# A recurrent attention state and an MLP on one core: the last 64 rows of x multiplied on the two row halves of TensorE

## The chip, the cores and the metric

The kernel runs on one core of one Trainium2 chip. The metric is device time in microseconds (us). Before the change the median of 3 runs is 756.64 us.

## What is computed

For 4 x 8 batch-head pairs a 40 x 40 state is updated 768 times; its outputs, put side by side, are x with 3072 tokens and 320 features. An MLP follows.

```python
for t in range(S):                       # S = 768, state is B x H x 40 x 40
    y[:, :, t] = einsum('bhd,bhde->bhe', rt, state)
    Sa = einsum('bhde,bhe->bhd', state, at)
    state = state * wt - outer(Sa, bt) + outer(vt, kt)
x = y.transpose(0, 2, 1, 3).reshape(3072, 320)
h = x @ w_in                             # 320 -> 2048
sp = maximum(h, 0) + log1p(exp(-abs(h)))
out = (h * erf(sp)) @ w_out              # 2048 -> 320
```

## The kernel before

**The recurrence** is cut into chunks of 32 steps: 48 chunk steps in all (2 groups of 16 heads, 24 chunks each), computed with small matrix products. A chunk step issues on TensorE, under the names used below: A (line 484, 104 rows contracted, 64 output columns), two sets of transposes (502, 664), Z (639, 96 x 32), U (648, 32 x 32), one more transpose (673), PQ (682, 104 x 64), MY (693 and 697, 64 x 40 and 40 x 40, on the row halves and the column halves of the array, into the two PSUM banks of `my`). For each group of four chunks there are W and DAD (595, 32 x 32). All of these but the transposes use a part of the array, and many of them share it. Each instruction carries the shape of tile into which it divides the array: 128 x 64, 128 x 32, 64 x 64 or 32 x 32 for A and PQ, Z, MY, and U, W and DAD; the whole 128 x 128 for the transposes and for the MLP's products. "Small tile" below means any shape other than 128 x 128.

**The MLP** runs in 12 tiles of 256 tokens (`load_x`), each in 8 pieces n (`mm1`, `unit`, `post`). A piece is a pair of blocks of 128 columns of w_in: 256 of the 2048 columns. So there are 96 pieces and 192 blocks. x and w_in are split in a high and a low part (`xh` + `xl`, `wih` + `wil`), and a block sums three products: high by high, high w by low x, low w by high x. The 320 rows of x are two sets of 128 and a rest of 64. For the rest, `wir` (128 x 2048) holds the high part of w_in's last 64 rows in partitions 0 to 63 and the low part in 64 to 127, and `xh[2]` holds the rest of x twice, so one full matmul gives high by high and low by high together. `xl[2]` is the low part of the rest; its partitions 64 to 127 are zeros, written once at the start (line 420).

So a block (line 869) is 8 matmuls of 128 x 128 weights by 256 columns, in one accumulation:

```python
ops = [(s.wih[0], xh[0], 128), (s.wih[1], xh[1], 128), (s.wir, xh[2], 128), (s.wih[0], xl[0], 128),
       (s.wih[1], xl[1], 128), (s.wir, xl[2], 128), (s.wil[0], xh[0], 128), (s.wil[1], xh[1], 128)]
```

The sixth, `wir` by `xl[2]`, is the one with zeros in half of its rows. The pieces take the two PSUM banks `ph[0]` and `ph[1]` in turn; a copy (`hc`, mostly ScalarE, line 376) takes the bank to `h` in SBUF. After Tanh, Ln, Exp and Gelu on ScalarE and products on VectorE, `post` multiplies by w_out (line 924): 4 products of 128 x 128 by 320 columns for each piece, 384 in all, into `po`. They are fp32, and the trace has two records for each of them, and also for each fp32 product of the recurrence; the matmuls of line 869 are float32r and have one.

**The order** of all work is a table of numbers, `ORDER`, with a second one, `ENGINES`, that gives each operation its engine. `Plan.add` lists operations with what they read and write, `emission` issues them in the table's order, and each engine runs its own instructions in that order. On TensorE blocks of line 869, products of line 924 and the small tiles of the recurrence stand mixed. After the program proper stands a second, sequential form of the recurrence, which runs only if a flag is set; it isn't in the trace.

Of the kernel before, what the change touches and what calls it, by code (L numbers as in the profile page):

```python
# [1056 lines left out]
```

## Time and profile before

| what | value |
|---|---|
| three runs | 752.92, 757.29, 756.64 us; median 756.64 us |
| the profiled execution | 755.08 us |
| its span, first to last instruction | 752.8 us |
| mean granted clock of TensorE over the span | 0.985 of full speed |
| busy share of the span | PE 95%, PEld 76%, DVE 85%, ACT 79% |

PE stands for TensorE's matmuls, PEld for its weight loads, DVE for VectorE, ACT for ScalarE. In a row, "start, duration" of a matmul cover its whole way through the array, and consecutive matmuls overlap: what one of them costs TensorE is read from the distance of one end to the next (start plus duration), not from its own duration. Where several like matmuls stand in one row, the row's end is that of the last of them.

### The profile page before, as it was taken

Reading aid. Unit: us, or ns where it says so; the run is one execution under the profiler, and the core shown is the slowest. Engines: PE = TensorE matmul, PEld = TensorE weight load, DVE = VectorE, ACT = ScalarE, POOL = GpSimd, SP = SyncE. Lnnn points to the kernel's source line nnn. Section 1 sums busy time; section 2 is a strip of 40 time slices with the busy share of each in tenths; the row PEclk is TensorE's granted clock in tenths of the full one; section 3 lists DMA queues with packets and bytes.
Section 4 is the critical chain, followed back from the end, with each engine's and each line's share of the span. In section 5 each row is a group of like instructions: output and inputs, shape, how many; then the busy total and the mean of one; then the engine's idle time right before and its main releaser. Section 6 shows DMA issues by size and latency. Waiting matters only on the chain.

```text
span 752.8 us, 32777 instructions
## 1 busy us (share of the span) xinstructions
PE 717.6 (95%) x14131; PEld 574.0 (76%) x14131; DVE 637.2 (85%) x1444; ACT 594.2 (79%) x1179; POOL 3.9 (1%) x12
## 2 busy tenths in 40 slices
...
GB/s 256 180 132 139 197 243 127 142 134 121 127 163 102 138 151 108 132 137 108 140 119 135 123 110 141 131 124 131 122 118 116 110 128 91 100 57 58 26 19 21
DMA packets 157523, 93.31 MB, mean 124 GB/s; under 512 B 107612, under 2 KB 141084, under 8 KB 157372
## 3 DMA queue, kind: packets, MB, share of 16 engines
...
q14 instruction: 38, 0.31, 0.2%
...
## 4 chain that ended last, share of the span: by engine, by line
PE 73%; DVE 9%; ACT 7%; DMA 5%; issue 3%; SPq 1%; DVEq 0%; ACTq 0%
PE po L924 25%; PE ph L869 19%; PE my L693 4%; PE pQ L682 3%; PE pA L595 3%; PE pA L484 3%; PE ph L424 2%; PE my L648 2%; ACT r L877 2%; PE my L639 2%; PE pA L502 2%; PE pQ L664 2%; ACT l L877 2%; PE my L697 2%; SPq L382 1%
## 5 line engine op out<-in xcount | busy, mean ns | idle before, releaser
L924 PE MATMUL po<-wo,h 128*128 128x320 f32 x768 | 267.2, 458 | 2.9 <-issue 2.1
L924 PEld LDWEIGHTS po<-wo,h 128*128 128x128 f32 x768 | 128.0, 192 | 34.5 <-issue 2.8
L869 PE MATMUL ph<-xh,wih 128*128 128x256 f32 x384 | 114.4, 379 | 1.1 <-ACT xh L376 0.6
L877 ACT ACTIVATE l<-l 128x512 f32<-128x512 f32 x192 | 111.2, 624 | 2.5 <-DVE nd L902 1.6
L869 PEld LDWEIGHTS ph<-xh,wih 128*128 128x128 f32 x384 | 69.7, 190 | 25.8 <-ACT xh L376 1.1
L869 PE MATMUL ph<-xl,wih 128*128 128x256 f32 x384 | 77.3, 283 | 0.0
L869 PE MATMUL ph<-xh,wil 128*128 128x256 f32 x384 | 77.0, 282 | 0.0
L902 DVE TENSOR_TENSOR nd<-l,r 128x512 f32<-128x512 f32 x96 | 64.0, 685 | 11.3 <-ACT r L877 9.7
L376 ACT COPY h<-ph 128x512 f32<-128x512 f32 x87 | 50.4, 583 | 26.3 <-PE ph L869 22.1
L914 DVE TENSOR_TENSOR l<-l,r 128x512 f32<-128x512 f32 x96 | 64.3, 682 | 1.1 <-ACT l L877 0.2
L903 DVE SCALAR_TENSOR_TENSOR r<-nd,r 128x512 f32<-128x512 f32 x96 | 64.7, 682 | 0.4
L915 DVE SCALAR_TENSOR_TENSOR h<-l,h 128x512 f32<-128x512 f32 x96 | 64.4, 682 | 0.5
L877 ACT ACTIVATE l<-h 128x512 f32<-128x512 f32 x96 | 58.2, 628 | 5.7 <-DVE h L378 4.2
L869 PEld LDWEIGHTS ph<-xh,wil 128*128 128x128 f32 x384 | 59.7, 191 | 0.0
L869 PEld LDWEIGHTS ph<-xl,wih 128*128 128x128 f32 x384 | 59.3, 190 | 0.1
L877 ACT ACTIVATE r<-r 128x512 f32<-128x512 f32 x96 | 55.7, 625 | 0.5
L869 PE MATMUL ph<-xl,wir 128*128 128x256 f32 x192 | 54.5, 284 | 0.0
L869 PE MATMUL ph<-xh,wir 128*128 128x256 f32 x192 | 54.1, 282 | 0.0
L877 ACT ACTIVATE r<-l 128x512 f32<-128x512 f32 x96 | 53.7, 618 | 0.2
L491 DVE TENSOR_TENSOR Zs<-pA,tri 64x256 f32<-64x256 f32 x96 | 40.6, 423 | 13.5 <-PE pA L484 6.5
L693 PE MATMUL my<-Vu,sg 64*40 64x72 f32 x1536 | 46.2, 230 | 3.8 <-DVE Vu L685 2.4
L693 PEld LDWEIGHTS my<-Vu,sg 64*40 64x40 f32 x1536 | 34.6, 114 | 11.8 <-DVE Vu L685 3.9
...
## 6 DMA issues: line engine op xcount, KB each, us to landing
...
```

The lines of the kernel that those rows point to most:

```text
L376: self.nc.scalar.copy(o, i)
L484: nc.tensor.matmul(pa[i % 2 * 64:i % 2 * 64 + 64, i // 4, i // 2 % 2], bk[:, i].rearrange("p a b -> p (a b)"), ab[:, :, i], start=True, st ...
L491: P.add("Am", "DVE", lambda e, x=x, xs=xs: nc.vector.tensor_tensor(out=zx[64:128, x], in0=pz[xs], in1=s.tri[xs, None, :].to_broadcast([64, ...
L595: nc.tensor.matmul(pw[js, i, ts], l[js, i], r[js, i, ts], start=True, stop=True)
L693: nc.tensor.matmul(my[h * 64:h * 64 + 40, x, j], sg[xs, j, h], vu[xs, j // 2 * 2 + h, j % 2], start=True, stop=False)
L869: nc.tensor.matmul(ph[:, j * 256:j * 256 + 256], a[:k, fs], b[:k], start=(m == 0), stop=(m == 7))
L877: self.P.add(name, "ACT", lambda e: nc.scalar.activation(out=o, in_=i, **kw), rd, wr + ["act"], pr, 0.62)
L902: P.add("nd", [("DVE", 0.69)], lambda e, r=r, l=l, nd=nd: s.eng(e).tensor_tensor(out=nd, in0=l, in1=r, op=ALU.mult), [("l", il), ("r", ir) ...
L903: P.add("rho", "DVE", lambda e, r=r, nd=nd: nc.vector.scalar_tensor_tensor(out=r, in0=nd, scalar=2 * C4, in1=r, op0=ALU.add, op1=ALU.mult) ...
L914: P.add("E", [("DVE", 0.69)], lambda e: s.eng(e).tensor_tensor(out=l, in0=l, in1=r, op=ALU.mult), [("r", ir)], [("l", il)], pr)
L915: P.add("G", "DVE", lambda e: nc.vector.scalar_tensor_tensor(out=h, in0=l, scalar=-1.0, in1=h, op0=ALU.add, op1=ALU.mult), [("l", il)], [( ...
L924: nc.tensor.matmul(po, h[:, bs], s.wo[:, f], start=(f == 0), stop=(f == 15))
```

## The change

`wir` is laid out anew: of the 8 pieces of a token tile, even ones keep high in partitions 0 to 63 and low in 64 to 127, odd ones have low above and high below. `xl[2]` is computed in all 128 partitions, since `xr` holds the rest of x twice, and the zeros of line 420 are gone. A block then has 7 matmuls (line 872 of the changed kernel), and after each even piece an operation of its own, `mk` (line 882), adds high w by low x of the rest for the even piece and the next odd one: 4 matmuls of 64 rows, 128 weight columns and 256 moving columns, in turn on array rows 0 to 63 into `ph[0]` and on rows 64 to 127 into `ph[1]`. Their tile is 64 x 128. `mk` closes the sum in `ph[0]` and opens the one in `ph[1]`.

```diff
@@ host @@
-    o["moe_w_in3"] = np.concatenate([wi[256:320, :1024], wi[256:320, 1024:]])
+    w3 = wi[256:320].reshape(64, 4, 2, 256)
+    o["moe_w_in3"] = np.concatenate([w3[:, :, x].reshape(64, 1024) for x in range(2)])
@@ start @@
-        for j in range(len(s.XL)):
-            P.add("zxl", "ACT", lambda e, j=j: nc.scalar.copy(s.XL[j][2][64:128], zero[64:128, :256]), s.TK, [("xl", j, 2)], -50, 0.36)
@@ weights @@
-                P.add("wr0", "ACT", lambda e, f=f, xs=xs, qs=qs: nc.scalar.copy(s.wir[0:64, qs], f[xs]), [kf], [kr + ("h",)], pr, 0.6)
+                P.add("wr0", "ACT", lambda e, f=f, xs=xs, qs=qs: nc.scalar.copy(s.wir[xs, qs], f[xs]), [kf], [kr + ("h",)], pr, 0.6)
...
@@ load_x @@
-            P.add("xl", [("DVE", 0.42)], lambda e, k=k, raw=raw, n=n: s.eng(e).tensor_tensor(out=xl[k][:n], in0=raw[:n], in1=xh[k][:n].bitcast(F32), op=ALU.subtract), ...
+            P.add("xl", [("DVE", 0.42)], lambda e, k=k, raw=raw: s.eng(e).tensor_tensor(out=xl[k], in0=raw, in1=xh[k].bitcast(F32), op=ALU.subtract), ...
@@ mm1 @@
+        col = lambda t, j: t % 2 * 1024 + t // 2 * 256 + j * 128
+        t, odd = n % 8, n % 2 == 1
...
-                ops = [(s.wih[0], xh[0], 128), (s.wih[1], xh[1], 128), (s.wir, xh[2], 128), (s.wih[0], xl[0], 128), (s.wih[1], xl[1], 128), (s.wir, xl[2], 128), (s.wil[0], xh[0], 128), (s.wil[1], xh[1], 128)]
-                for m, (a, b, k) in enumerate(ops):
-                    nc.tensor.matmul(ph[:, j * 256:j * 256 + 256], a[:k, fs], b[:k], start=(m == 0), stop=(m == 7))
+                ops = [(s.wih[0][:, fs], xh[0]), (s.wih[1][:, fs], xh[1]), (s.wir[:, cs], xh[2]), (s.wih[0][:, fs], xl[0]), (s.wih[1][:, fs], xl[1]), (s.wil[0][:, fs], xh[0]), (s.wil[1][:, fs], xh[1])]
+                for m, (a, b) in enumerate(ops):
+                    nc.tensor.matmul(ph[:, j * 256:j * 256 + 256], a, b, start=(m == 0 and not odd and j == 0), stop=(m == 6 and odd and j == 1))
...
+        if not odd:
+
+            def mk(e):
+                for j in range(2):
+                    for x in range(2):
+                        xs, cs = slice(x * 64, x * 64 + 64), slice(col(t + x, j), col(t + x, j) + 128)
+                        nc.tensor.matmul(s.ph[x][:, j * 256:j * 256 + 256], s.wir[xs, cs], xl[2][xs], start=(x == 1 and j == 0), stop=(x == 0 and j == 1))
+
+            P.add("mk", "PE", mk, xks + wkr(t) + wkr(t + 1) + ["phw"] * (n == 0), [("ph", 0), ("ph", 1)], pr, 0.35)
@@ ORDER and ENGINES, both written anew @@
-2 3 28 29 30 31 32 33 34 35 36 37 38 39 40 41 42 43 44 45 46 47 48 49 50 51 52 53 54 55 56 57 58 59 60 61 62 63 64 65 66 67 68 69 70 6 27 11 7 71 72 73 74 75 76 77 13 78 9 4 17 15
...
```

The order on TensorE, before, at a usual place in the second half: `ph_163` and `ph_164` are `ph[0]` and `ph[1]`, `po_165` and `po_166` the two banks of `po`. A whole block stands between a product of line 924 and transposes of line 664.

```order
L924 MATMUL po_166<-wo,h 128x320
L869 MATMUL ph_164<-xh_0_152,wih_126 128x256
L869 MATMUL ph_164<-xh_1_153,wih_127 128x256
L869 MATMUL ph_164<-xh_2_154,wir 128x256
L869 MATMUL ph_164<-xl_0_158,wih_126 128x256
L869 MATMUL ph_164<-xl_1_159,wih_127 128x256
L869 MATMUL ph_164<-xl_2_160,wir 128x256
L869 MATMUL ph_164<-xh_0_152,wil_128 128x256
L869 MATMUL ph_164<-xh_1_153,wil_129 128x256
L664 MATMUL pQ<-ident,MT_111 104x104 x4
L639 MATMUL my<-Zm_77,Zs_70 32x40 x16
```

In the changed kernel, at a like place of TensorE, `mk` (line 882) stands alone between a product of w_out (line 936 there) and the next block:

```order
L936 MATMUL po_165<-wo,h 128x320
L882 MATMUL ph_163<-xl_2_157,wir 128x256
L882 MATMUL ph_164<-xl_2_157,wir 128x256
L882 MATMUL ph_163<-xl_2_157,wir 128x256
L882 MATMUL ph_164<-xl_2_157,wir 128x256
L872 MATMUL ph_164<-xh_0_149,wih_126 128x256
L872 MATMUL ph_164<-xh_1_150,wih_127 128x256
```

The sixth matmul of a block is gone, and four of another tile shape stand between two runs of whole-array work. At another place of the changed kernel's TensorE, `mk` stands ahead of a small tile of the recurrence, here U of line 648:

```order
L872 MATMUL ph_163<-xh_1_153,wil_129 128x256
L936 MATMUL po_166<-wo,h 128x320
L664 MATMUL pQ<-ident,MT_111 104x104 x4
L639 MATMUL my<-Zm_77,Zs_70 32x40 x16
L936 MATMUL po_166<-wo,h 128x320
L882 MATMUL ph_163<-xl_2_160,wir 128x256
L882 MATMUL ph_164<-xl_2_160,wir 128x256
L882 MATMUL ph_163<-xl_2_160,wir 128x256
L882 MATMUL ph_164<-xl_2_160,wir 128x256
L648 MATMUL my<-zt_110,Tb_83 32x40 x16
L936 MATMUL po_166<-wo,h 128x320
```

Here the array's shape changes from 128 x 128 to 64 x 128, to 32 x 32 and back, where without `mk` it would go to 32 x 32 and back.

Counted over the whole order of TensorE, in matmuls whose tile shape differs from that of the one before:

| change of shape | before | changed |
|---|---|---|
| 128 x 128 to a small tile of the recurrence | 197 | 197 |
| small tile to another small tile of the recurrence | 60 | 55 |
| small tile of the recurrence to a matmul of mm1 or w_out | 153 | 157 |
| small tile of the recurrence to a transpose or other whole-array matmul | 44 | 51 |
| into `mk`, from 128 x 128 / from a small tile | | 46 / 2 |
| `mk` to a matmul of mm1 or w_out / to another whole-array matmul / to a small tile | | 28 / 7 / 13 |
| sum | 454 | 556 |

## Rows read from the trace of the kernel before

**Rows 1.** The page, busy time of TensorE, VectorE and ScalarE (share of span, instructions).
```profile
PE 717.6 (95%) x14131; PEld 574.0 (76%) x14131; DVE 637.2 (85%) x1444; ACT 594.2 (79%) x1179; POOL 3.9 (1%) x12
```

**Rows 2.** Busy time of each engine in three stretches of the span.
```profile
core 0: us, PE busy (x) PEld busy (x) DVE busy (x) ACT busy (x) POOL busy (x), PEclk, DMA share, GB/s
0.00:172.00 172.00, 147.63 (x3104) 106.69 (x3104) 143.35 (x326) 99.06 (x228) 3.90 (x12) 0.95 0.65 171
172.00:700.00 528.00, 522.21 (x10786) 430.01 (x10783) 458.76 (x1062) 455.41 (x890) 0.00 (x0) 1.00 0.50 120
700.00:753.00 53.00, 47.76 (x247) 37.29 (x245) 35.12 (x58) 39.69 (x63) 0.00 (x0) 0.98 0.04 15
```

**Rows 3.** Groups by line and shape: out<-in xcount | busy us, mean ns | idle before.
```profile
L869 PE MATMUL ph<-xl,wir 128*128 128x256 f32 x192 | 54.5, 284 | 0.0
...
L869 PEld LDWEIGHTS ph<-xl,wir 128*128 128x128 f32 x192 | 36.5, 190 | 0.0
...
L697 PEld LDWEIGHTS my<-Rt,Sm 40*40 40x40 f32 x1536 | 38.5, 114 | 0.0
...
L376 ACT COPY h<-ph 128x512 f32<-128x512 f32 x87 | 50.4, 583 | 26.3 <-PE ph L869 22.1 <-DVE wo L785 3.4
```

**Rows 4.** Timeline of PE, a block between w_out products: start us, duration us, what.
```profile
498.05 0.43 PE L924 MATMUL po<-wo,h 128*128 128x320 f32 x1
498.08 0.64 PE L869 MATMUL ph<-xh,wih 128*128 128x256 f32 x2
498.56 0.28 PE L869 MATMUL ph<-xh,wir 128*128 128x256 f32 x1
498.68 0.40 PE L869 MATMUL ph<-xl,wih 128*128 128x256 f32 x2
498.92 0.28 PE L869 MATMUL ph<-xl,wir 128*128 128x256 f32 x1
499.04 0.40 PE L869 MATMUL ph<-xh,wil 128*128 128x256 f32 x2
499.27 0.43 PE L924 MATMUL po<-wo,h 128*128 128x320 f32 x1
```

**Rows 5.** Timeline of PE, MY (two eights of each line).
```profile
552.38 0.32 PE L693 MATMUL my<-Vu,sg 64*40 64x72 f32 x8
552.51 0.25 PE L697 MATMUL my<-Rt,Sm 40*40 40x32 f32 x8
552.58 0.31 PE L693 MATMUL my<-Vu,sg 64*40 64x72 f32 x8
552.72 0.25 PE L697 MATMUL my<-Rt,Sm 40*40 40x32 f32 x8
```

**Rows 6.** Timeline of PE just after it: the first w_out record behind MY.
```profile
552.90 0.54 PE L924 MATMUL po<-wo,h 128*128 128x320 f32 x1
```

**Rows 7.** Timeline of PE, a block behind W (32 x 32).
```profile
538.03 0.80 PE L595 MATMUL pA<-T,Ap 32*32 32x16 f32 x74
538.75 0.50 PE L869 MATMUL ph<-xh,wih 128*128 128x256 f32 x2
...
539.57 0.40 PE L869 MATMUL ph<-xh,wil 128*128 128x256 f32 x2
```

**Rows 8.** Timeline of PE, the first record of Z behind a transpose.
```profile
317.26 0.34 PE L664 MATMUL pQ<-ident,MT 104*104 104x104 f32 x2
317.53 0.22 PE L639 MATMUL my<-Zm,Zs 96*32 96x40 f32 x1
```

**Rows 9.** Timeline of PE, the first record of Z (128 x 32) behind DAD (32 x 32).
```profile
542.43 0.35 PE L595 MATMUL pA<-Tb,W 32*32 32x16 f32 x20
542.70 0.22 PE L639 MATMUL my<-Zm,Zs 96*32 96x40 f32 x1
```

**Rows 10.** Timeline of PE, the first transpose behind W; then behind a block.
```profile
372.99 0.31 PE L595 MATMUL pA<-T,Ap 32*32 32x16 f32 x16
373.23 0.30 PE L664 MATMUL pQ<-ident,MT 104*104 104x104 f32 x1
...
400.85 0.40 PE L869 MATMUL ph<-xh,wil 128*128 128x256 f32 x2
401.08 0.25 PE L664 MATMUL pQ<-ident,MT 104*104 104x104 f32 x1
```

More of the change, by code (lines that the diff above doesn't have):

```diff
@@ L15 @@
 ORDER = tuple(int(x) for x in """
[122 rows of a table removed]
[123 rows of a table added]
 """.split())
 ENGINES = "".join("""
-SSVVGVGGAVAGAGGAAAGAVVVVGAAAPPPPPPPPPPPPPPPPPPPPPPPPPPPPPPPPPPPPPPPPPPPPPPPPPPPPPPPPPPPPPPPPPPPPPPPPPPPPPPPPPPPPPPPPPPPPPPPPPPPPPPPPPPPPPPPPPPPPPPPPPPPPPPPPPPSAVVVVSVSSVPVVPVAAVAVV
-PAVPAVVPVVVPAVVPVSVSSVPVVPAVAAVVVPVVPAVVPAVVPAVVPVSVSSVPVVPASVSSVPVVPAVAAAAVVAVVPAVPAVVPAVVPAVVPVSVVVAPAPASVVVAPAPASVVVAPAPASVVVAPAPASVVVAPAPVSVVVAPAPASVVVAPAPVSVVVAPAPASVVVAAAPVVP
-AASVVVAAAPAAPAASVVVSVVVSVVVSVVVSVVVSVVVSVVVSVVVSVVVSVVVSAVVAVSVSSVPVVSSPVSVSSVPVVSSPASVSSVPVVSSPASVSSVPVVSSPVSSSSSSAAPAPAAVAAPAPAPVPVVSSSSSSAAPVPVAAAAPAPAPVPVVSSSSSSAVPAPAAAAAPAPAP
@@ L143 @@
-VPVVSSSSSSVAPAPAAAAVPAPAPVPVVSSSSSSSSAAVVVVVVVVVVVVVVVVVVVVVVVVVVVVSSSSVPPPPAPPPPVSAVSAVSSAVPPAAPPAAPPAAPPAAAAAAAAAAAAAAAAVVVVVVVVAAAAAPPAAPPAAPPAAVVPPPPPPAAVVPPPPVVPPPPVVPPPPSAVVA
-VSVSSVPVVSSPVSVSSVPVVSSPVSVSSVPVVSSPASVSSVPVVSSPASSSSSSAAPAPASAVAPVPAPVPVVSSSSSSVAPAPAASAAPAPAPVPVVSSSSSSAAPAPAAAVAPAPAPVPVVSSSSSSAAPAPAVAAAPAPAPVPVVSSSSSSSSAAVVVVVVVVVVVVVVVVVVVVV
-VVVVVVVSSSSVPPPPAPPPPVSAVSAVSSAVAAAAAAAAAAAAAAVVVVVVVVAAAAAPPAAPPAAPPAAVVPPPPPPAAVVPPPPVVPPPPVVPPPPASASAAAAAAAAAAAAAAVVVVVVVVAAAAAPPAAPPAAPPAAVVPPPPPPAAVVPPPPVVPPPPVVPPPPSAVVVVSVSS
@@ L146 @@
-VPVVSSPASVSSVPVVSSPASVSSVPVVSSPASVSSVPVVSSPASSSSSSVAAPAPAAAAAPVPAPVPVVSSSSSSAAPAPAAAAAPAPAPVPVVSSSSSSVVPAPAASASPAPAPVPVVSSSSSSAAPVPAAVAAPAPAPVPVVSSSSSSSSAAVVVVVVVVVVVVVVVVVVVVVVVVV
-VVVSSSSVPPPPAPPPPVSVVSVVSSVVAAAAAAAAAAAAAAVVVVVVVVAAAAAPPAAPPAAPPAAVVPPPPPPAAVVPPPPVVPPPPVVPPPPASASAAAAAAAAAAAAAAVVVVVVVVAAAAAPPAAPPAAPPAAVVPPPPPPAAVVPPPPVVPPPPVVPPPPSAVVVVSVSSVPVV
-SSPASVSSVPVVSSPASVSSVPVVSSPASVSSVPVVSSPASSSSSSVAVPVPVSAAVPAPVPVPVVSSSSSSAAPAPASAAAPAPAPVPVVSSSSSSVAPAPVSSAAPVPAPVPVVSSSSSSAAPAPAAAAAPAPAPVPVVSSSSSSSSAAVVVVVVVVVVVVVVVVVVVVVVVVVVVVS
@@ L149 @@
-SSSVPPPPAPPPPVSAVSVVSSAVAAAAAAAAAAAAAAVVVVVVVVAAAAAPPAAPPAAPPAAVVPPPPPPAAVVPPPPVVPPPPVVPPPPASASAAAAAAAAAAAAAAVVVVVVVVAAAAAPPAAPPAAPPAAVVPPPPPPAAVVPPPPVVPPPPVVPPPPSAVVVVSVSSVPVVSSPA
-SVSSVPVVSSPASVSSVPVVSSPASVSSVPVVSSPASSSSSSVAVPAPAVVSVPAPVPVPVVSSSSSSAAPAPAAAASPAPAPVPVVSSSSSSAAPAPASASAPAPAPVPVVSSSSSSVAPVPAAASAPAPAPVPVVSSSSSSSSAAVVVVVVVVVVVVVVVVVVVVVVVVVVVVSSSSV
-PPPPVPPPPVSAVSAVSSAVAAAAAAAAAAAAAAVVVVVVVVAAAAAPPAAPPAAPPAAVVPPPPPPAAVVPPPPVVPPPPVVPPPPVSASAAAAAAAAAAAAAAVVVVVVVVAAAAAPPAAPPAAPPAAVVPPPPPPAAVVPPPPVVPPPPVVPPPPSAVVAVSVSSVPVVSSPASVSS
@@ L152 @@
-VPVVSSPASVSSVPVVSSPASVSSVPVVSSPASSSSSSVVAPVPAAVAAPVPAPVPVVSSSSSSAAPAPASAAAPAPAPVPVVSSSSSSAAPVPASVSAPAPAPVPVVSSSSSSAVPAPAASAVPAPAPVPVVSSSSSSSSAAVVVVVVVVVVVVVVVVVVVVVVVVVVVVSSSSVPPPP
-VPPPPVSVVSAVSSAVAAAAAAAAAAAAAAVVVVVVVVAAAAAPPAAPPAAPPAAVVPPPPPPAAVVPPPPVVPPPPVVPPPPASVSAAAAAAAAAAAAAAVVVVVVVVAAAAAPPAAPPAAPPAAVVPPPPPPAAVVPPPPVVPPPPVVPPPPSAVVAVSVSSVPVVSSPASVSSVPVV
-SSPASVSSVPVVSSPASVSSVPVVSSPASSSSSSVAVPVPAVVAAPAPAPVPVVSSSSSSAAPAPAAAAAPAPAPVPVVSSSSSSVAPAPAVVSAPAPAPVPVVSSSSSSAAPAPAAASAPAPAPVPVVSSSSSSSSAAVVVVVVVVVVVVVVVVVVVVVVVVVVVVSSSSVPPPPVPPP
@@ L155 @@
-PVSAVSVVSSVVAAAAAAAAAAAAAAVVVVVVVVAAAAAPPAAPPAAPPAAVVPPPPPPAAVVPPPPVVPPPPVVPPPPASASAAAAAAAAAAAAAAVVVVVVVVAAAAAPPAAPPVAPPAAVVPPPPPPAAVVPPPPVVPPPPVVPPPPSAVVAVSVSSVPVVSSPVSVSSVPVVSSPA
-SVSSVPVVSSPASVSSVPVVSSPASSSSSSVVAPVPASVVAPAPVPVPVVSSSSSSAAPAPAAASAPAPAPVPVVSSSSSSAAPAPAAASAPAPAPVPVVSSSSSSAVPAPVAVAAPVPAPVPVVSSSSSSSSAAVVVVVVVVVVVVVVVVVVVVVVVVVVVVSSSSVPPPPAPPPPVSV
-VSVVSSVVAAAAAAAAAAAAAAVVVVVVVVAAAAAPPAAPPAAPPAAVVPPPPPPAAVVPPPPVVPPPPVVPPPPASASAAAAAAAAAAAAAAVVVVVVVVAAAAAPPVAPPAAPPAAVVPPPPPPAAVVPPPPVVPPPPVVPPPPSAVVVVSVSSVPVVSSPVSVSSVPVVSSPASVSS
@@ L158 @@
-VPVVSSPASVSSVPVVSSPASSSSSSVAVPAPAVASVPAPVPVPVVSSSSSSAAPAPAAAAAPAPAPVPVVSSSSSSAAPAPAAASSPAPAPVPVVSSSSSSVVPVPVASSVPAPAPVPVVSSSSSSSSAAVVVVVVVVVVVVVVVVVVVVVVVVVVVVSSSSVPPPPAPPPPVSVVSVV
-SSAVAAAAAAAAAAAAAAVVVVVVVVAAAAAPPAAPPAAPPAAVVPPPPPPAAVVPPPPVVPPPPVVPPPPASASAAAAAAAAAAAAAAVVVVVVVVAAAAAPPAAPPAAPPAAVVPPPPPPAAVVPPPPVVPPPPVVPPPPSAVVAVSVSSVPVVSSPVSVSSVPVVSSPASVSSVPVV
-SSPASVSSVPVVSSPASSSSSSVAAPVPVVVAVPAPAPVPVVSSSSSSVAPAPAAAAAPAPAPVPVVSSSSSSAAPAPAVAVSPAPAPVPVVSSSSSSVAPAPAAVAAPAPAPVPVVSSSSSSSSAAVVVVVVVVVVVVVVVVVVVVVVVVVVVVSSSSVPPPPVPPPPVSVVSAVSSVV
@@ L161 @@
-AAAAAAAAAAAAAAVVVVVVVVAAAAAPPAAPPAAPPAAVVPPPPPPAAVVPPPPVVPPPPVVPPPPVSASAAAAAAAAAAAAAAVVVVVVVVAAAAAPPAAPPAAPPAAVVPPPPPPAAVVPPPPVVPPPPVVPPPPSAVVVVSVSSVPVVSSPASVSSVPVVSSPASVSSVPVVSSPA
-SVSSVPVVSSPASSSSSSVVAPAPVVAAAPAPAPVPVVSSSSSSAVPAPAVAASPAPVPVPVVSSSSSSVVPVPVSVAVPVPAPVPVVSSSSSSAAPAPAAAAAPAPAPVPVVSSSSSSSSAAVVVVVVVVVVVVVVVVVVVVVVVVVVVVSSSSVPPPPVPPPPVSVVSVVSSVVAAAA
-AAAAAAAAAAVVVVVVVVAAAAAPPAAPPAAPPAAVVPPPPPPAAVVPPPPVVPPPPVVPPPPVSVSAAAAAAAAAAAAAAVVVVVVVVAAAAAPPVAPPAAPPVAVVPPPPPPAAVVPPPPVVPPPPVVPPPPSSSSSSVAAPVPVSASAPAPVPVPVVSSSSSSAVPAPVVVVSPVPV
@@ L164 @@
-PVPVVSSSSSSVVPVPAAAVAPAPAPVPVVSSSSSSVAPAPAVAASPAPAPVPVVSSSSVPVVSVVSVVSSVVAAAAAAAAAAAAAAVVVVVVVVAAAAAPPVAPPAAPPVAVVPPPPPPAAVVPPPPVVPPPPVVPPPPVSVSAAAAAAAAAAAAAAVVVVVVVVAAAAAPPVAPPVAP
-PVAVVPPPPPPAAVVPPPPVVPPPPVVPPPPAAAAAAAAAAAAAAVVVVVVVVAAAAAVVPPPPVVPPPPVVPPPPVVPPPPVSAS
+SSVVGVGAGAAVAAVVAVAVGVVGVAPPPPPPPPPPPPPPPPPPPPPPPPPPPPPPPPPPPPPPPPPPPPPPPPPPPPPPPPPPPPPPPPPPPPPPPPPPPPPPPPPPPPPPPPPPPPPPPPPPPPPPPPPPPPPPPPPPPPPPPPPPPPPPPPPPSAVVVVSVSSVPVVPAAAVAVVPV
+VPAVVPVVVPAVVPVSVSSVPVVPAAVVAVVPAVPVVVPAVVPAVVPVSVSSVPVVPASVSSVPVVPAAVVAAAAAVVPAVPAVVPAVVPAVVPVSVVVAPAPASVVVAPAPVSVVVAPAPASVVVAPAPASVVVAPAPASVVVAPAPASVVVAPAPASVVVAPVPVSVVVAAAPAVPAA
@@ new lines @@
+SVVVAAAPAAPAASVVVSVVVSVVVSVVVSVVVSVVVSVVVSVVVSVVVSVVVSAVVVVSVSSVPVVSSPVSVSSVPVVSSPASVSSVPVVSSPASVSSVPVVSSPVSSSSSSAAPAPAVAAAPAPAPVPVVSSSSSSVVPAPVAAAAPVPAPVPVVSSSSSSAVPAPAAAAAPAPAPVP
+VVSSSSSSAVPAPAVAAAPAPAPVPVVSSSSSSSSAAVVVVVVVVVVVVVVVVVVVVVVVVVVVVSSSSVPPPPAPPPPVSAVSAVSSAVPPPVAPPAAPPPAAPPAAAAAAAAAAAAAAAAVVVVVVVVAAAAAPPPAAPPAAPPPAAVVPPPPPPAAVVPPPPVVPPPPVVPPPPSAV
+VAVSVSSVPVVSSPASVSSVPVVSSPASVSSVPVVSSPASVSSVPVVSSPASSSSSSAAPAPAAVVAPVPVPVPVVSSSSSSVAPAPASAAAPAPAPVPVVSSSSSSAAPAPAAAAAPAPAPVPVVSSSSSSAVPAPAVAAAPAPAPVPVVSSSSSSSSAAVVVVVVVVVVVVVVVVVVV
@@ new lines @@
+VVVVVVVVVSSSSVPPPPAPPPPVSVVSAVSSAVAAAAAAAAAAAAAAVVVVVVVVAAAAAPPPAAPPAAPPPAAVVPPPPPPAAVVPPPPVVPPPPVVPPPPVSVSAAAAAAAAAAAAAAVVVVVVVVAAAAAPPPAAPPAAPPPAAVVPPPPPPAAVVPPPPVVPPPPVVPPPPSAVV
+VVSVSSVPVVSSPASVSSVPVVSSPVSVSSVPVVSSPASVSSVPVVSSPASSSSSSVAVPAPAAAAAPAPVPVPVVSSSSSSAAPAPAAAVAPAPAPVPVVSSSSSSAAPAPASVAVPAPAPVPVVSSSSSSAVPAPAAAAAPAPVPVPVVSSSSSSSSAAVVVVVVVVVVVVVVVVVVV
+VVVVVVVVVSSSSVPPPPVPPPPVSAVSAVSSVVAAAAAAAAAAAAAAVVVVVVVVAAAAAPPPAAPPAAPPPAAVVPPPPPPAAVVPPPPVVPPPPVVPPPPASASAAAAAAAAAAAAAAVVVVVVVVAAAAAPPPAAPPAAPPPAAVVPPPPPPAAVVPPPPVVPPPPVVPPPPSAVV
@@ new lines @@
+AVSVSSVPVVSSPVSVSSVPVVSSPASVSSVPVVSSPASVSSVPVVSSPASSSSSSVAAPAPVAAAAPVPAPVPVVSSSSSSAAPAPAASAAPAPAPVPVVSSSSSSVAPAPVAVASPVPVPVPVVSSSSSSVAPAPAASAAPAPAPVPVVSSSSSSSSAAVVVVVVVVVVVVVVVVVVV
+VVVVVVVVVSSSSVPPPPAPPPPVSVVSVVSSVVAAAAAAAAAAAAAAVVVVVVVVAAAAAPPPAAPPAAPPPAAVVPPPPPPAAVVPPPPVVPPPPVVPPPPVSASAAAAAAAAAAAAAAVVVVVVVVAAAAAPPPAAPPAAPPPAAVVPPPPPPAAVVPPPPVVPPPPVVPPPPSAVV
+VVSVSSVPVVSSPVSVSSVPVVSSPASVSSVPVVSSPASVSSVPVVSSPASSSSSSVVAPVPVSAASPAPAPVPVVSSSSSSAAPAPAVAASPAPAPVPVVSSSSSSAVPAPAAVAAPAPAPVPVVSSSSSSVAPAPAAAAAPVPAPVPVVSSSSSSSSAAVVVVVVVVVVVVVVVVVVV
@@ new lines @@
+VVVVVVVVVSSSSVPPPPVPPPPVSAVSVVSSAVAAAAAAAAAAAAAAVVVVVVVVAAAAAPPPAAPPAAPPPAAVVPPPPPPAAVVPPPPVVPPPPVVPPPPASASAAAAAAAAAAAAAAVVVVVVVVAAAAAPPPAAPPAAPPPAAVVPPPPPPAAVVPPPPVVPPPPVVPPPPSAVV
+VVSVSSVPVVSSPASVSSVPVVSSPASVSSVPVVSSPASVSSVPVVSSPASSSSSSVAVPVPAVAAAPVPAPVPVVSSSSSSAAPAPAAAAAPVPAPVPVVSSSSSSAAPAPAVSVAPAPAPVPVVSSSSSSVAPVPASAVSPAPVPVPVVSSSSSSSSAAVVVVVVVVVVVVVVVVVVV
+VVVVVVVVVSSSSVPPPPVPPPPVSAVSAVSSVVAAAAAAAAAAAAAAVVVVVVVVAAAAAPPPAAPPAAPPPAAVVPPPPPPAAVVPPPPVVPPPPVVPPPPVSASAAAAAAAAAAAAAAVVVVVVVVAAAAAPPPAAPPAAPPPAAVVPPPPPPAAVVPPPPVVPPPPVVPPPPSAVV
@@ new lines @@
+VVSVSSVPVVSSPASVSSVPVVSSPASVSSVPVVSSPASVSSVPVVSSPASSSSSSVAVPVPAAAAAPVPAPVPVVSSSSSSAAPAPASVAAPAPAPVPVVSSSSSSVAPVPAASAVPAPVPVPVVSSSSSSAAPAPAVAVVPAPAPVPVVSSSSSSSSAAVVVVVVVVVVVVVVVVVVV
+VVVVVVVVVSSSSVPPPPVPPPPVSVVSVVSSAVAAAAAAAAAAAAAAVVVVVVVVAAAAAPPPAAPPAAPPPAAVVPPPPPPAAVVPPPPVVPPPPVVPPPPVSASAAAAAAAAAAAAAAVVVVVVVVAAAAAPPPVAPPAAPPPAAVVPPPPPPVAVVPPPPVVPPPPVVPPPPSAVV
+VVSVSSVPVVSSPASVSSVPVVSSPVSVSSVPVVSSPASVSSVPVVSSPASSSSSSVAAPVPAAVAAPVPAPVPVVSSSSSSAAPAPAAAASPAPAPVPVVSSSSSSAAPAPASAASPAPAPVPVVSSSSSSVAPVPVAAAAPAPAPVPVVSSSSSSSSAAVVVVVVVVVVVVVVVVVVV
@@ new lines @@
+VVVVVVVVVSSSSVPPPPAPPPPVSVVSVVSSVVAAAAAAAAAAAAAAVVVVVVVVAAAAAPPPAAPPAAPPPAAVVPPPPPPAAVVPPPPVVPPPPVVPPPPASVSAAAAAAAAAAAAAAVVVVVVVVAAAAAPPPAAPPAAPPPAAVVPPPPPPAAVVPPPPVVPPPPVVPPPPSAVV
+AVSVSSVPVVSSPVSVSSVPVVSSPASVSSVPVVSSPASVSSVPVVSSPVSSSSSSVAAPVPAAAVVPAPAPVPVVSSSSSSAAPAPAAAAAPAPAPVPVVSSSSSSAAPAPASASSPAPAPVPVVSSSSSSVAPVPAAAAAPAPAPVPVVSSSSSSSSAAVVVVVVVVVVVVVVVVVVV
+VVVVVVVVVSSSSVPPPPVPPPPVSAVSVVSSVVAAAAAAAAAAAAAAVVVVVVVVAAAAAPPPAAPPAAPPPAAVVPPPPPPAAVVPPPPVVPPPPVVPPPPVSASAAAAAAAAAAAAAAVVVVVVVVAAAAAPPPAAPPAAPPPAAVVPPPPPPAAVVPPPPVVPPPPVVPPPPSAVV
@@ new lines @@
+AVSVSSVPVVSSPVSVSSVPVVSSPASVSSVPVVSSPASVSSVPVVSSPASSSSSSVAAPAPASAVVPVPAPVPVVSSSSSSAAPAPAAASAPAPAPVPVVSSSSSSAVPAPVSAAAPVPAPVPVVSSSSSSAVPAPVSAAAPAPVPVPVVSSSSSSSSAAVVVVVVVVVVVVVVVVVVV
+VVVVVVVVVSSSSVPPPPVPPPPVSAVSAVSSVVAAAAAAAAAAAAAAVVVVVVVVAAAAAPPPAAPPVAPPPAAVVPPPPPPAAVVPPPPVVPPPPVVPPPPVSASAAAAAAAAAAAAAAVVVVVVVVAAAAAPPPAAPPAAPPPVAVVPPPPPPAAVVPPPPVVPPPPVVPPPPSAVV
+VVSVSSVPVVSSPASVSSVPVVSSPASVSSVPVVSSPASVSSVPVVSSPASSSSSSVAVPVPAVASAPAPAPVPVVSSSSSSAAPAPAAVSSPAPAPVPVVSSSSSSVVPVPVVAVSPVPAPVPVVSSSSSSAAPAPAVAAAPAPAPVPVVSSSSSSSSAAVVVVVVVVVVVVVVVVVVV
```

16 lines of the change are left out of this document (10 added, 6 removed), and 244 rows, old and new, of the table ORDER.

## Prediction

> **What bounds the kernel now.** I read the busy times first, then by stretch, then the timeline around single blocks. On the page TensorE is busy for 717.6 of 752.8 us, ahead of VectorE with 637.2 and ScalarE with 594.2 [rows 1]. By stretch this becomes sharp [rows 2]: from 172 to 700 us TensorE is busy for 522.2 of 528 us at the full granted clock, while VectorE has 69 us and ScalarE 73 us to spare. There a microsecond of TensorE work is a microsecond of time. In the first 172 us TensorE idles for 24 us, and in the last 53 us for 5.
>
> The groups by line can't tell what a matmul costs: `wir` by `xl[2]` has a mean of 284 ns [rows 3], but neighbours overlap in the array. Ends do. In the timeline a w_out record ends at 498.05 + 0.43 = 498.48 and the eighth matmul of the block behind it at 499.04 + 0.40 = 499.44: 0.96 us for eight, 0.12 each. The next w_out record ends at 499.70, 0.26 later [rows 4]. No step within whole-array work costs extra, though the types change.
>
> A change of tile shape does. Behind MY, whose last record ends at 552.97 [rows 5], the first w_out record ends at 553.44 [rows 6]: 0.47 instead of 0.26, **0.2 us more**. A block behind W takes 538.83 to 539.97, that is 1.14 instead of 0.96 [rows 7], so 0.18 more. In the other direction the first record of Z ends 0.15 behind the last of the transposes (317.60 to 317.75) [rows 8]. It does so behind DAD too (542.78 to 542.92, 0.14) [rows 9], and that place matters: 32 x 32 to 128 x 32 alters the rows of the tile alone and costs as much. A transpose behind W ends 0.23 behind it (373.30 to 373.53), behind a block 0.08 (401.25 to 401.33) [rows 10]: 0.15 more, with 104 weight columns instead of 128. What grows with the columns looks like a weight load: 190 ns recorded for 128 columns, 114 for 40 [rows 3]. Within one shape it hides under the matmul before; across a change it is bare.
>
> **The change part by part.**
>
> *Removed:* 192 full matmuls, 192 x 0.12 = 23.0 us. This is real TensorE work, on the path wherever TensorE bounds.
>
> *Added:* 48 `mk` of four matmuls. Do the row halves run side by side? No row shows 64 x 128, but MY uses rows and columns in halves. A turn of MY's 8 + 8 records takes 0.2 us (ends at 552.76 and 552.97) [rows 5]. By the 0.26 us of 320 columns, 72 columns cost 0.06 and 32 cost 0.026, so one after the other they would need 8 x 0.086 = 0.69 us. They run some 3.4 at a time. Column halves alone give at most 2, so row halves run side by side, weight loads included, and the second of two comes about 0.2 / 16 = 0.01 us after the first. A pair in `mk` thus costs 0.12 + 0.01, two pairs 0.26.
>
> The entry into `mk`: no row shows a change to 64 x 128. The ends are 0 (no change needed when the columns stay whole) and 0.2 us (the price of 128 weight columns behind any other shape). I take 0.2: `mk` loads 128 columns, and rows 9 show that a change in rows alone is paid. `mk` is then 0.46 us, 48 of them 22.1 us.
>
> The exit: in the order 28 `mk` are followed by blocks or w_out (0.2 each), 7 by a transpose or such (0.15), 13 by a small tile, whose entry would be paid behind whole-array work too. That is 5.6 + 1.1 = 6.7 us. So an `mk` between whole-array work costs 0.66 us where four matmuls of 0.48 us went: it loses 0.18. Ahead of a small tile it gains 0.02.
>
> One rule bears on this. In the Trainium skill, "TensorEngine Tiling (Array Packing)", section Tiling Modes, a change of the tiling mode drains the engine, while a change of the tile within a mode doesn't; 64 x 128 is listed as a mode of its own. The trace agrees for all shapes that it has (0.15 to 0.2 us), and has none at 64 x 128. By this rule the entry and the exit are paid, as taken above.
>
> *Moved:* outside `mk` the new order has 4 more exits to blocks or w_out (0.8 us), 7 more to transposes (1.1) and 8 more entries into small tiles (55 + 13 - 60, at 0.15: 1.2), 3.1 us together.
>
> *At nothing:* `xl[2]` grows from 64 to 128 partitions and not in columns, on VectorE with its spare 69 us; two ScalarE copies at the start go, where ScalarE works 99 of 172 us [rows 2]. The copy of `ph[0]` now waits for `mk`, which stands up to a few products later than the end of its piece. Behind the copy ScalarE's queue waits; but those copies already wait 26 us in all without TensorE starving, so I charge nothing. If that cover went, it would show as the last rival says. `mk` needs `ph[1]` free at the place where the odd block needed it before, no earlier than that by more than its own length.
>
> The sum for TensorE: -23.0 + 22.1 + 6.7 + 3.1 = **+8.9 us**. Between 172 and 700 us nothing absorbs it. In the first 172 us a tenth of the `mk` stand (5 of 48 come ahead of the ninth MY in the order), beside idle time, so I take off 1 us. The profiled execution took 755.08 us, 1.6 below the median of 756.64 of the three runs; with +8 it would be **763 us**, 1.05% more than itself and 0.8% more than the median. A measurement tells this kernel from no change from about 1% on (7.6 us), so the forecast lies on that line.
>
> **The rivals.**
>
> *No change of shape (faster).* If 64 x 128 needs no change, because the columns aren't split, entry and exit vanish: `mk` costs 0.26, 48 of them 12.5 us, and the sum is -23.0 + 12.5 + 3.1 = -7.4 us, 747.7 us. For it: no small tile in the trace keeps all 128 columns. Against it: rows 9, where columns stay and rows change at the full price. It decides from an entry plus exit under 0.1 us on. Chance 0.12. This is also what the Trainium skill would give by "TensorE: Matmul & The Clock Gate", Part 3, which says that weight loads overlap running matmuls if the row groups differ, and names no price of a change; no run here shows it for 64 rows.
>
> *The new order starts better (no measurable difference).* TensorE idles 24 us before 172 us [rows 2], and the order was found anew. If it fills 6 us of that, the time is 757. For it: that idle time; against it: VectorE is busy for 143 of those 172 us, and the order of the stages is the same. Chance 0.2.
>
> *The halves don't run side by side.* Each `mk` then takes 0.22 more, 10.6 us: 774 us. Against it rows 5. Chance 0.05.
>
> *The copies come late.* `ph[0]` is held until `mk` has run; if the next even block waits 0.15 us for it each time, 48 x 0.15 = 7 us more: 770 us. For it: ScalarE waits for line 869 already, 22 us [rows 3]. Chance 0.08.
>
> **How the numbers follow.** The forecast has 0.55 and lies on the line of 1%, so I split it: 0.28 slower, 0.27 same. The first rival gives 0.07 faster and 0.05 same; the second 0.04 faster, 0.13 same and 0.03 slower; the last two 0.13 slower. Faster 0.11, same 0.45, slower 0.44. The range goes from 752 (the better start in full, with cheaper entries) to 771 (late copies); the first rival and unshared halves lie outside with about 2 in 10.
>
> **What would show it.** In the profile after, the ends of `mk`'s four records: first 0.32 behind whole-array work, then 0.01, 0.12, 0.01; the block or w_out record behind it 0.2 late. If the first comes 0.12 behind and the next is not late, the first rival holds. If the four come 0.12 apart, the halves don't run side by side. TensorE's busy time from 172 us on should still be near all of the time. If the time falls although the `mk` cost what I say, the start moved: TensorE's idle time ahead of 172 us would shrink below the 24 us of before.

## The result, and the profile after

The changed kernel takes **763.44 us** (median of 4 runs, 762.31 to 765.16), the kernel before 756.84 us beside it (median of 4, 752.92 to 757.29). The ratio is **1.0115**, with an interval of 1.0067 to 1.0163: some 1% slower. The ratio, here and below, compares the fast runs alone and is not the quotient of the two medians, which is 1.0087 here, or 6.6 us. Run again beside other kernels (e8) it gave 1.0109 (1.0030 to 1.0188). The profiled execution took 765.16 us, with a span of 763.3 us.

The page of the changed kernel, its busy line and its chain, answers to [rows 1]:

```profile
PE 729.9 (96%) x14131; PEld 566.2 (74%) x14131; DVE 646.7 (85%) x1472; ACT 587.8 (77%) x1158; POOL 2.1 (0%) x9
...
PE 79%; ACT 6%; DVE 6%; DMA 5%; issue 3%; SPq 1%; ACTq 0%; DVEq 0%
```

TensorE issues as many matmuls as before (192 records less in the blocks, 192 more in `mk`), and is busy for 12.3 us longer (7.8 us in the profile of the same kernel in e8). The windows of the changed kernel answer to [rows 2] (columns as there):

```profile
0.00:172.00 172.00, 148.74 (x3007) 104.19 (x3008) 140.71 (x324) 92.68 (x212) 2.09 (x9) 0.92 0.64 167
172.00:700.00 528.00, 522.98 (x10838) 418.09 (x10835) 463.74 (x1076) 448.62 (x873) 0.00 (x0) 1.00 0.50 119
700.00:763.00 63.00, 58.14 (x295) 43.89 (x294) 42.24 (x74) 46.45 (x73) 0.00 (x0) 0.99 0.09 29
```

From 172 to 700 us TensorE is as full as before (522.98 against 522.21 of 528 us): no waits came in, so what the kernel lost there is work, or time that counts as work. TensorE is nearly full in that window either way and only comes to the end later: the last window ends at 763 us instead of 753. In the first 172 us the changed kernel got through 3007 matmuls instead of 3104, at a granted clock of 0.92 instead of 0.95. That difference is not the change's: the same kernel in e8 did 3149 there at 0.94 and had a span of 757.4 us, and another kernel with the same order (e4 below) did 3225 at 0.97. So the 10.5 us between the two profiled spans are not the size of the change; the ratio is.

The groups of the changed kernel by line and shape answer to [rows 3]; L882 is `mk`:

```profile
L882 PE MATMUL ph<-xl,wir 64*128 64x256 f32 x192 | 24.7, 334 | 0.0
...
L882 PEld LDWEIGHTS ph<-xl,wir 64*128 64x128 f32 x192 | 14.7, 187 | 13.3 <-issue 10.3
...
L378 ACT COPY h<-ph 128x512 f32<-128x512 f32 x83 | 48.3, 582 | 24.1 <-PE ph L872 18.2 <-PE ph L882 5.4
```

By this view the change looks like a gain: 24.7 us busy for `mk`, where the same products took 54.5 us in the group that is gone. As ahead of the change, the group can't tell what a matmul costs; the ends can. The timeline of TensorE in the changed kernel around an `mk` that stands between a w_out record and a block, from short windows (a window takes in only the records that touch it, so neighbours come apart):

```profile
433.47 0.43 PE L936 MATMUL po<-wo,h 128*128 128x320 f32 x1
433.83 0.39 PE L882 MATMUL ph<-xl,wir 64*128 64x256 f32 x2
434.06 0.28 PE L882 MATMUL ph<-xl,wir 64*128 64x256 f32 x2
434.27 0.39 PE L872 MATMUL ph<-xh,wih 128*128 128x256 f32 x1
```

The w_out record ends at 433.90. The first pair of `mk` ends at 433.83 + 0.39 = 434.22, 0.32 behind it; the second at 434.06 + 0.28 = 434.34, 0.12 later; the first record of the block at 434.66, another 0.32 later instead of the 0.12 of [rows 4]. So the second of a pair is nearly free and the two changes of shape are not. Over all 48 `mk` the trace gives these medians from end to end: first record 0.313, second 0.003, third 0.114, fourth 0.004, together **0.434 us**; the exit is 0.198 over the usual step to a block, 0.197 to a w_out record and 0.14 to a transpose. Another neighbour, from the same view of the changed kernel:

```profile
511.64 0.49 PE L648 MATMUL my<-zt,Tb 32*32 32x40 f32 x32
512.07 0.51 PE L882 MATMUL ph<-xl,wir 64*128 64x256 f32 x4
```

Behind U, which is a small tile itself, `mk` ends at 512.58, 0.45 behind the last record of U (512.13): the entry costs as much as behind whole-array work.

### The profile page after: what moved, and what is told of

It reads as the page before. It is cut to its first block, busy times and chain, and to the rows that moved or that the text cites. A ratio compares the mean times of both kernels' runs of the same rounds, so it can differ in the third digit from the quotient of the medians.

```text
span 763.3 us, 32733 instructions
## 1 busy us (share of the span) xinstructions
PE 729.9 (96%) x14131; PEld 566.2 (74%) x14131; DVE 646.7 (85%) x1472; ACT 587.8 (77%) x1158; POOL 2.1 (0%) x9
## 4 chain that ended last, share of the span: by engine, by line
PE 79%; ACT 6%; DVE 6%; DMA 5%; issue 3%; SPq 1%; ACTq 0%; DVEq 0%
PE po L936 27%; PE ph L872 20%; PE my L693 4%; PE pQ L682 4%; PE pA L595 3%; PE ph L882 2%; PE pA L484 2%; PE ph L424 2%; PE my L648 2%; PE my L639 2%; PE pA L502 2%; PE pQ L664 2%; PE my L697 2%; ACT l L889 1%; PE pQ L673 1%
## 5 line engine op out<-in xcount | busy, mean ns | idle before, releaser
L872 PE MATMUL ph<-xh,wih 128*128 128x256 f32 x384 | 108.6, 364 | 1.2 <-ACT xh L378 0.8
L872 PEld LDWEIGHTS ph<-xh,wih 128*128 128x128 f32 x384 | 67.0, 192 | 22.0 <-ACT xh L378 1.1
L378 ACT COPY h<-ph 128x512 f32<-128x512 f32 x83 | 48.3, 582 | 24.1 <-PE ph L872 18.2
L872 PE MATMUL ph<-xh,wir 128*128 128x256 f32 x192 | 54.5, 284 | 0.0
L378 ACT COPY Zm<-MT 40x320 f32<-40x320 f32 x67 | 30.6, 457 | 21.4 <-DVE MT L700 20.4
```

The source lines that it names most:

```text
L378: self.nc.scalar.copy(o, i)
L872: nc.tensor.matmul(ph[:, j * 256:j * 256 + 256], a, b, start=(m == 0 and not odd and j == 0), stop=(m == 6 and odd and j == 1))
```

## The experiments

The ratios are to the kernel before, run beside each group on the same chip (before: 753.90 us median of 25 for e1 to e4, 753.95 of 6 for e5 to e8, 752.35 of 7 for e9 and e10). My theory: TensorE bounds; `mk` pays an entry and an exit and so loses more than the 192 matmuls give; the new order outside `mk` adds some changes of shape of its own. Rivals: the loss is the order's alone; or it comes from waits (the copy of `ph[0]`, held by `mk`).

**e1_whole_array_mk.** The order of the changed kernel, with `mk` as four matmuls of the whole array (the lower half of `xl[2]` zero, the weights laid out as before).

```diff
-    nc.tensor.matmul(s.ph[x][:, j * 256:j * 256 + 256], s.wir[xs, cs], xl[2][xs], ...)
+    nc.tensor.matmul(s.ph[x][:, j * 256:j * 256 + 256], s.wir[:, cs], xl[2], ...)
...
```

Expected: 

> The changed kernel in its own order, with mk as four whole-array matmuls (128 rows, the lower 64 of x's low part zero, layout of w as before): the same work as before, no 64 x 128 tile. My theory (the change of shape is what costs): each mk takes 4 x 0.12 = 0.48 us where it took 0.43, +2.4 us over 48, and the exits behind mk (28 at 0.2, 7 at 0.14) go, -6.6: 4 us below the changed kernel, 759 us, ratio to before 1.003. Rival (the price is in the waits: both banks opened by one operation, the copy of ph[0] held until mk has run): no gain, 763 us.

Measured: 757.71 us, ratio 1.0052 (1.0015 to 1.0088). Its timeline of TensorE shows `mk` (L887 there) ahead of a block:

```profile
516.29 0.64 PE L887 MATMUL ph<-xl,wir 128*128 128x256 f32 x4
516.77 0.40 PE L877 MATMUL ph<-xh,wih 128*128 128x256 f32 x2
```

Ends at 516.93 and 517.17: 0.24 for two, no step. Over all 48, the four of `mk` end 0.118, 0.120, 0.119 and 0.120 behind the record ahead of each, 0.476 together. The kernel with twice the matmul work in the same place is the faster one, by 1.0115 - 1.0052 = 0.6%, 4 to 5 us; with both intervals that can be anything from near nothing to 9 us. The ends give 48 x (0.434 - 0.476) + 6.5 of exits = 4.5 us, which agrees. That is the price of the packing; the 0.5% that is left belongs to the rest.

**e2_blocks_of_eight.** The tables of the changed kernel (ORDER and ENGINES), with the blocks of before and an empty `mk`.

```diff
-    ops = [..., (s.wih[1][:, fs], xl[1]), (s.wil[0][:, fs], xh[0]), ...]
+    ops = [..., (s.wih[1][:, fs], xl[1]), (s.wir[:, cs], xl[2]), (s.wil[0][:, fs], xh[0]), ...]
...
     def mk(e):
-        for j in range(2): ...
+        pass
```

Expected: 

> The blocks of before (eight matmuls each, mk empty) in the order of the changed kernel: the order alone. My theory: the new order has 11 more exits and 8 more entries outside mk, +3 us: 759 to 760 us, as e1. Rival (the new order is as good or starts better): 754 to 757 us.

Measured: 759.69 us, ratio 1.0064 (1.0022 to 1.0106). It has the arithmetic of before and differs in the two tables alone, so **the new tables cost some 5 us by themselves** (1.7 to 8.0 by the interval); e1, whose `mk` also changes no shape, agrees (1.1 to 6.6). Counted in the order, both have 475 changes of tile shape where before has 454: 21 more, at 0.15 to 0.2 us each 3 to 4 us. That these 21 are the whole of it is not shown: ENGINES is new too, and VectorE has 1472 instructions in e2 where before has 1444.

**e3_no_mk.** The changed kernel without the products of `mk`.

```diff
...
     def mk(e):
-        for j in range(2): ...
+        pass
```

Expected: 

> The changed kernel without mk's matmuls (high w by low x of the last 64 rows is left out of the sum). My theory: 48 x 0.43 = 20.7 us of mk and 6.6 us of exits go, 27 us below the changed kernel: 736 us. If mk also costs by waits (both banks, late copies), clearly less, under 733 us. If its time lay beside other engines' limits, more, over 740 us.

Measured: 753.64 us, ratio 0.9958 (0.9917 to 0.9998). Only 1.5%, some 11.5 us (7 to 17 by the intervals), came back of the 27 us that `mk` takes with its exits (20.8 + 6.5, by the ends above): a miss. The window from 172 to 700 us, the longest waits of TensorE in it (what waits and for what: us in total, times, longest), and the chain on the page, in e3:

```profile
172.00:700.00 528.00, 514.80 (x10672) 416.18 (x10671) 467.44 (x1086) 451.43 (x879) 0.00 (x0) 0.99 0.50 120
```

```profile
PE pA L595 <- issue: 5.4, 5, 1.7
PE pA L595 <- DVE T L586: 2.5, 3, 1.8
```

```profile
PE 61%; DVE 14%; ACT 10%; DMA 6%; issue 5%; SPq 2%; DVEq 0%; ACTq 0%
```

With `mk` away TensorE is busy for 514.80 instead of 522.98 us there, and W (L595) stands and waits, in part for its input from VectorE; in the changed kernel the longest of these sums in that stretch is 1.0 us. TensorE's share of the chain falls from 79% to 61%, and VectorE's rises from 6% to 14%. So another chain, that of the recurrence, lies close below TensorE: work taken from TensorE gives back less than its size. A part of what is missing is the clock: TensorE's granted clock is 0.982 in the mean of nine executions of e3, against 0.987 in eight of the changed kernel. By my estimate, 0.005 of some 755 us, that is 4 us. Whether the waits brought the clock down was not tried.

**e4_one_half_at_a_time.** The loops of `mk` exchanged, so that two matmuls of the same row half follow each other.

```diff
-    for j in range(2):
-        for x in range(2):
+    for x in range(2):
+        for j in range(2):
```

Expected: 

> mk's four matmuls in the order upper half twice, then lower half twice: only the middle two can run side by side. My theory: one more step of 0.11 us in each mk, +5.3 us: 769 us, and ends in the trace at 0.31, 0.11, 0.00, 0.11. Rival (the halves don't run side by side, or their weight loads don't): no change, 763 us.

Measured: 761.55 us, ratio 1.011 (1.004 to 1.018), the time of the changed kernel: a miss. Its window at the start, and its `mk` between a w_out record and a block, from the timeline of TensorE in short windows:

```profile
0.00:172.00 172.00, 151.11 (x3225) 108.06 (x3229) 150.74 (x343) 97.95 (x224) 2.09 (x9) 0.97 0.66 175
```

```profile
422.17 0.43 PE L936 MATMUL po<-wo,h 128*128 128x320 f32 x1
422.53 0.39 PE L882 MATMUL ph<-xl,wir 64*128 64x256 f32 x2
422.75 0.29 PE L882 MATMUL ph<-xl,wir 64*128 64x256 f32 x2
422.97 0.39 PE L872 MATMUL ph<-xh,wih 128*128 128x256 f32 x1
```

Ends at 422.60, 422.92, 423.04 and 423.36: 0.32, 0.12 and 0.32 again. With either order of issue the four end in two pairs and cost the same. The ends in a profile are modelled, so they alone would not show it; the time agrees with them, though not by much: had the halves queued up behind each other as I expected, the time would have been some 5 us above that of the changed kernel, a ratio of 1.018, which is the upper end of the interval. The starts show what happened. In e4 the matmul that completes `ph[0]`, and signals its copy, is issued second; in all 32 `mk` whose records carry that signal it is the third to start, as in the changed kernel, where it is issued third. So TensorE took the first matmul of the other row half ahead of the second of the same half.

**e5_mk_in_old_order.** The order and the engines of before, with `mk` directly behind each even piece; what could not stay where it was by its dependences was moved back. The edit to the changed kernel is the two tables; on TensorE it reads at an even piece and the odd one behind it (the block's line is 827 here, that of `mk` 837):

```order
L827 MATMUL ph_163<-xh_1_150,wil_129 128x256
L837 MATMUL ph_163<-xl_2_157,wir 128x256
L837 MATMUL ph_164<-xl_2_157,wir 128x256
L837 MATMUL ph_163<-xl_2_157,wir 128x256
L837 MATMUL ph_164<-xl_2_157,wir 128x256
L827 MATMUL ph_164<-xh_0_149,wih_126 128x256
```

Expected: 

> The change with as little of the new order as it allows: the order of before, mk put right behind each even piece, and what may not stand ahead of it moved back. By the prices of changes of shape TensorE's work is 3 us above before: 757 to 759 us if work alone decides. Rival (waits: mk needs both banks at one place, so the copies of the odd pieces have to be done earlier than in the old order, and TensorE's queue stands behind it): far more, up to 780 us, with idle time of TensorE in front of mk.

Measured: 779.13 us, ratio 1.0365 (1.0279 to 1.0451). Here the waits did come: TensorE is busy for 507.74 of the 528 us from 172 to 700 us, and ScalarE's copies of `ph` wait for 48.6 us instead of the 26.3 of [rows 3]. The window, TensorE's longest waits for ScalarE in the same stretch, and the group of the copies in e5:

```profile
172.00:700.00 528.00, 507.74 (x10391) 403.94 (x10390) 438.32 (x1022) 435.83 (x856) 0.00 (x0) 0.99 0.49 116
```

```profile
PE my L594 <- ACT Zm L333: 3.6, 5, 1.3
PE pQ L637 <- ACT vt L333: 3.2, 6, 0.9
```

```profile
L333 ACT COPY h<-ph 128x512 f32<-128x512 f32 x87 | 50.2, 582 | 48.6 <-PE ph L827 35.9 <-PE ph L837 12.4
```

I read this at first as my last rival: `mk` (L837) holds the copy, the copy holds ScalarE's queue, and TensorE waits for what stands behind it. That reading is tried in e10.

**e6_before_reordered, e7_after_reordered.** Both kernels with an order from a search of my own, which knew the measured prices of a change of shape: 450 changes for the kernel before, 504 for the changed one. The edit is the table ORDER alone:

```diff
-ORDER = ...
+ORDER = ...
```

Expected of e6: 

> The kernel before with another order of the same operations (found with the measured prices of a change of shape: 450 changes for 454, TensorE's work 2 us less, and less idle time planned). If TensorE's work alone decides: 752 to 755 us. If the idle time of the first 172 us and the waits can be ordered away: 725 to 745 us.

Expected of e7: 

> The changed kernel with an order found in the same way: 504 changes of shape for 556, TensorE's work 9.6 us less than in its own order and equal to e6. My theory (the loss is changes of shape, not the row halves as such): the same time as e6 within 1%, 8 us or more below the changed kernel. Rival (mk costs by holding both banks, in any order): 5 us or more above e6.

Measured: 820.40 us, ratio 1.0867 (1.0768 to 1.0966) for e6, and 810.52 us, 1.0789 (1.0685 to 1.0892) for e7. Both missed by far, and neither says anything on `mk`. TensorE's longest waits in e7 between 172 and 700 us:

```profile
PE pA L550 <- issue: 12.7, 9, 2.4
PE my L648 <- DVE Vu L640: 5.3, 4, 2.2
```

Fewer changes of shape than in the changed kernel (504 against 556), and far more waits: W alone (L550) stands for 12.7 us, and TensorE is busy for 495.48 of the 528 us. The granted clock is lower too, 0.96 in that stretch instead of 1.00. An order that is good by the prices of TensorE alone is not good. What my search had wrong about when inputs arrive was not looked into further.

**e8_changed_again.** The changed kernel, unedited, as the measure for e5 to e7.

Expected: 

> The changed kernel as it is, beside the others on one chip: 1.01 times before, as first measured.

Measured: 760.43 us, ratio 1.0109 (1.0030 to 1.0188).

**e9_mk_split.** The last matmul of each even piece moved between the two pairs of its `mk`: no work more, two changes of shape more for each `mk`, 96 in all.

```diff
-    for m, (a, b) in enumerate(ops):
+    for m, (a, b) in enumerate(ops[:6] if j and not odd else ops):
...
     for j in range(2):
+        if j:
+            fs = slice(t * 256 + 128, t * 256 + 256)
+            nc.tensor.matmul(s.ph[0][:, 256:512], s.wil[1][:, fs], xh[1], start=False, stop=False)
         for x in range(2):
...
```

Expected: 

> The changed kernel in its own order, with the last matmul of the even piece's second block moved in between the two pairs of mk: the same matmuls, and in each mk one exit and one entry more. My theory: 48 x (0.2 + 0.2) = 19 us more than the changed kernel, 782 us, 1.036 times before; in the trace the moved matmul ends 0.32 behind the first pair, the second pair 0.31 behind it. Rival (a change of shape is hidden by other work, or costs only at the small tiles of the recurrence): 763 us.

Measured: 780.88 us, ratio 1.0399 (1.0368 to 1.0430). Against 1.011 that is 0.029, 22 us for 96 changes, **0.22 us each** (0.16 to 0.29 by the intervals). Its timeline of TensorE (L885 is `mk`, L882 the moved matmul), and its window:

```profile
517.43 0.38 PE L885 MATMUL ph<-xl,wir 64*128 64x256 f32 x2
517.74 0.38 PE L882 MATMUL ph<-xh,wil 128*128 128x256 f32 x1
518.05 0.38 PE L885 MATMUL ph<-xl,wir 64*128 64x256 f32 x2
```

```profile
172.00:700.00 528.00, 522.12 (x10491) 411.20 (x10486) 448.68 (x1043) 437.38 (x849) 0.00 (x0) 1.00 0.49 118
```

Ends at 517.81, 518.12 and 518.43: 0.31 and 0.31, where they would be 0.12 and 0.11 within one shape. 2 x 0.2 x 48 = 19 us by the ends, 22 us by the measured time; the 3 us between them lie within the intervals. TensorE stays as full as before (522.12 of 528): the price of a change counts as busy and not as waiting.

**e10_old_order_moved_blocks_of_eight.** The table of e5, with the blocks of before and an empty `mk` (the edit of e2).

Expected: 

> The order of e5 with the blocks of before (eight matmuls, mk empty). My theory of e5's loss (an even piece's copy, and so ScalarE's queue with the recurrence's copies in it, waits for mk, which stands later than the piece's own end): without mk the copies come as before, 755 to 760 us. Rival (what had to be moved back for mk's sake, the odd pieces behind the even ones, makes the loss by itself): 770 to 779 us.

Measured: 773.12 us, ratio 1.0279 (1.0249 to 1.0308). The copies' group in e10:

```profile
L332 ACT COPY h<-ph 128x512 f32<-128x512 f32 x87 | 50.1, 581 | 44.7 <-PE ph L832 44.2
```

No `mk`, and yet 44.7 us of waiting, and TensorE busy for only 508.24 of the 528 us: my reading of e5 fell. Counted in the order, e10 has no more changes of shape than before, so they are no part of its loss. 2.8 of e5's 3.65% come from what was moved back to make room for `mk`; `mk` itself adds 0.9%, with an uncertainty as large.

## Why the prediction was right, point by point

*TensorE bounds from 172 to 700 us, and what is added there is time.* Right: 522.98 of 528 us after; e9 adds 19 us of changes and the time rises by 22. In the other direction it doesn't hold (e3: 27 us less work, 11.5 us less time). That "a microsecond of TensorE work is a microsecond of time" held upwards only.

*Removed, 192 x 0.12 = 23.0 us.* Right as a step: e1 puts as many whole-array matmuls back, and their ends come 0.12 apart.

*A pair costs 0.12 + 0.01.* Right, 0.114 + 0.004. The rival that the halves don't run side by side (774 us) is refuted, by the ends and by the time.

*Entry 0.2, `mk` 0.46 us, 22.1 us in all.* The mechanism held, the size came out a little lower: the first record ends 0.313 behind its neighbour, 0.434 for an `mk`, 48 x 0.434 = 20.8 us. The term was 1.3 us too large. The rival without a change of shape (747.7 us) is refuted by the ends and, independently of them, by the time of e9. In the Trainium skill, "TensorEngine Tiling (Array Packing)", section Tiling Modes, a change of the tiling mode drains the engine. The trace agrees in that each way cost some 0.2 us here; it doesn't show that the engine drained.

*Exit 0.2 to a block or w_out, 0.15 to a transpose, nothing extra ahead of a small tile.* Right: 0.198, 0.197, 0.14. That the price grows with the weight columns is less sure than the prediction has it: Z, in tiles of 32 columns, pays 0.14 to 0.15 [rows 8] [rows 9], and a transpose, with 104, no more [rows 10].

*Moved elsewhere, 3.1 us, less 1 us in the first 172.* If anything too small: e1 and e2 put the two tables alone at 0.5 to 0.6%, 4 to 5 us, but 3.1 us lies within both intervals. What the new ENGINES table does was not priced at all. With the measured ends and 4.5 us for the tables the sum is -23.0 + 20.8 + 6.5 + 4.5 = +8.8 us. Measured were 1.0115 and 1.0109, that is +8.7 and +8.2 us (6.6 and 6.5 between the medians); +8 was predicted. So close a hit is partly luck: the term for `mk` was a little large and this one perhaps a little small, and the 8 us were put on a profiled execution that lay 1.6 us below the median.

*The copies charged at nothing.* Right in the order that the change has: they wait for 24.1 us, less than the 26.3 of [rows 3], 5.4 of it for `mk`. The rival of late copies did not come. In e5, with `mk` put into the order of before, they do wait longer and the kernel is 3.65% slower; e10 shows that 2.8% of that come from what had to be moved back, and not from `mk` holding the copies.

*The rival of a better start.* Not seen: e2, which has the new order and none of the packing, is slower than before, and TensorE idles for 25.1 us of its first 172 where before it was 24.4.

So the change packs the array and pays for it twice. The packing saves 0.24 us of matmul time per `mk` (four of 0.12 become two pairs) and costs two changes of shape, 0.4 us in the worst place. The order that had to be found anew keeps the waits out, with 21 changes more outside `mk`. Whether an order exists that has both few changes and few waits stays open: e6 and e7 failed at that, and no kernel here that computes all of it beat the one before.
